# A hybrid attention and MLP block: reordering the head, one load for two input tiles, and a constant folded into a statistics aggregation

## The chip, the cores and the metric

The kernel runs on one core of one Trainium2 chip. A core has a matrix engine (TensorE, "PE" in the profile), a vector engine (VectorE, DVE), a scalar engine (ScalarE, ACT), a general engine (GpSimd, POOL) and an engine that mostly issues transfers (SyncE, SP). They run their own instruction streams and wait for each other by semaphores. Matmuls write PSUM, which has eight banks; DMA engines move data between memory and the on-chip SBUF. The metric is the device time in microseconds of one execution; several are taken and the median is given.

## What is computed

The input x has 2048 rows of 448 numbers. Each row is normalized without learned weights. Two branches start from the normalized rows and both are added to x:

```python
xn = _layernorm(x, axis=-1)                       # (x - mean) / sqrt(var + 1e-5)
return x + _A_ref(xn, ...) + _B_ref(xn, w1, w2)

# A: attention without a softmax over positions, 16 heads of 28
q, k, v = split(xn @ wqkv)
pq, pk  = q @ w_phi, k @ w_phi                    # a 28 x 28 map for each head
phi     = concat(softmax(p), softmax(-p))         # 56 features, for q and for k
kv, z   = sum over rows of phi_k x v, and of phi_k
o       = (phi_q @ kv) / (phi_q . z + 1e-6)
A       = o @ wo
# B: an MLP with 1792 hidden units
B       = silu(xn @ w1) @ w2
```

All inputs and the output are bfloat16.

## The kernel before, in words

Rows are handled in 16 tiles of 128, and tiles in four chunks of 512 rows. TensorE works on halves: each "pair" is two matmuls with 64 contracted rows, one on the upper and one on the lower half of the array, into two neighbouring PSUM banks. Two banks make a slot; there are four, and a list `free` says which slot is taken next (`take`, `give`).

*How the order arises.* The function records operations: `pair` and `tpair` (L446, L459) for matmuls and transposes by matmul, `act` (L464) for ScalarE, `dve` and `pool` for the others, `load` (L477) for transfers. TensorE keeps the recorded order. Other operations are either marked as ordered or placed by `schedule`, a planner with costs and due times for each operation. A wait is put wherever one operation reads or overwrites what another wrote. `schedule` runs at build time; its numbers choose the order and are no measurement.

*The head.* Until the first tile is normalized, TensorE multiplies a matrix of ones (`warm`, ten pairs of 512 columns) into a spare slot. GpSimd writes those ones (L485) after another constant (L484). The input tiles x0 to x3 and `w1` come in on two issuing queues, SP's and ScalarE's; the order of issue is written out by hand (L515 to L524). `w_phi` comes in four small transfers into the block-diagonal tile `BD`, issued on SP after `w1` and ahead of everything in `load_bulk`. The transfers of `load_bulk` (raw query and key weights, value weights, x4 and so on, w2) each wait for the transfer four places before them in the list `chain`.

Tile t is normalized by `LN_st` (statistics, L573), `LN_ag` (aggregation to mean and variance, L577; `ve`, variance plus eps, L579; GpSimd's power of -1/2, `rstd`, L581) and `LN_b` (L596, in pieces). `LN_b` also writes a copy of the first 64 columns behind the tile (columns 448 to 512 of `xnd`), because the lower half of the array reads the columns one block of 64 further than the upper half. `X_tr` transposes the blocks by matmul and `X_ev` copies them out of PSUM, one half by ScalarE and one by DVE.

*The first chunk.* With tiles 0 and 1 transposed for some blocks (`WA`, `WB`), `f1a` and what follows it run the first hidden units of the MLP (F1A, F1B, unit 6) for rows 0 to 255. Then tiles 2 and 3 are transposed and `c0(i, ph)` runs the units for rows 256 to 511. Between them, `FT_tr` transposes the raw query and key weights (T0, T1) and `FM` multiplies them with `BD` (M0 to M3), so that `w_phi` is folded into the query and key weights; both use slot 3. `X_rest` transposes the two blocks of tiles 0 and 1 left over, also in slot 3. `F1silu` applies the activation and frees the slot. After that come the values `V(2)`, `V(0)`, the products with the folded weights (`QK`) and the first output matmuls of the MLP.

*The body* repeats this for chunks 1 to 3 with transposes by DMA. `KV` sums over rows in slot 3.

*The tail.* For tile pairs 0, 2, 4, 6 the MLP output was finished early and lies in `Ye`, in float32 with x added. For pairs 8 to 14 it stays in PSUM: `seed` copies x into the bank, `F2_ph` adds the MLP, and `WO_two` adds the attention output. `U(t)` (called by `nextu`) makes the attention output of a pair, DVE divides it, and a transposing DMA brings it to `oT` (in the profile this tile is part of `E`). `WO(t)` multiplies with `wo` for the early pairs; DVE then adds `Ye` (L833), and `store` writes the result.

Of the kernel before, what the change touches and what calls it, by code (L numbers as in the profile page):

```python
# [140 lines left out]
class _Prog:  # L141
# [97 lines left out]
    def _pass(self, when, shake=0):  # L239
# [46 lines left out]
        while done < n:  # L286
# [20 lines left out]
            if o.is_dma:  # L307
                issue_end = t + o.dur
                eng_free[o.eng] = issue_end
                if o.fixed is not None:  # L310
                    o.end = t + o.fixed
                else:
                    x0 = max(issue_end + 900.0, dma_free[0])
                    dma_free[0] = x0 + o.nbytes
                    o.end = dma_free[0] + 300.0 + o.late
# [14 lines left out]
def bass_parallel_sum__linear_kernel_hedgehog__dense_activation_silu__prompt_kernel(  # L330
# [21 lines left out]
    with es:  # L352
# [23 lines left out]
        st6 = sb("st6", [128, NT, 6], F32)  # L376
        mv = sb("mv", [128, NT, 2], F32)
        ve = sb("ve", [128, NT], F32)
# [8 lines left out]
        wsrc = hT[:, NH - 1, FT - 1, :]  # L387
        ones_bf = wsrc[:, 0:128]
# [84 lines left out]
        def service(nbytes, run):  # L473
            return nbytes / run * (12.0 + 0.0475 * run) / 16.0
# [10 lines left out]
        P.op("pool", 230, lambda e: e.memset(wsrc, 1.0), [], [wsrc], name="ones", ordered=True)  # L485
        P.op("pool", 290, lambda e: e.affine_select(ident[:], ones_bf, [[1, 128]], ALU.is_equal, 0.0, base=0,
                                                    channel_multiplier=-1), [ones_bf], [ident[:]], name="ident", ordered=True)
        def warm(n, sl=2, d=216.0):
            for i in range(n):
                pair([(bank(2 * sl + q)[:, 0:512], ones_bf[HALF[q], :], wsrc[HALF[q], :], True, True) for q in range(2)],  # L490
                     512, "warm", dur=d)

        P.unit = "warm"
        warm(10, d=427.0)


# [3 lines left out]
        def load_x(t0, t1, after=None, eng="sp"):  # L500
            load(x_sb[:, t0:t1, :], xv[:, t0:t1, :], (t1 - t0) * 128 * D * 2, (t1 - t0) * D * 2, f"x{t0}", issue=430, after=after,
                 eng=eng)
# [7 lines left out]
        def load_w1(b, eng):  # L510
            chain.append(load(w1_sb[:, 2 * b:2 * b + 2, :].rearrange("p h f -> p (h f)"), B_w1[b * 128:(b + 1) * 128, :],
                              128 * FF * 2, 2 * FF, f"w1{b}", eng=eng, issue=480))
# [7 lines left out]
        load_x(2, 3, eng="act")  # L520
        load_w1(2, "sp")
        for q, eng in enumerate(("sp", "act")):
            chain.append(load(w1_sb[HALF[q], 6, :], B_w1[384:448, q * 896:(q + 1) * 896], 64 * 896 * 2, 1792, f"w16{q}", eng=eng,
                              issue=480))  # L524
        load_x(3, 4, eng="act")
        P.op("pool", 300, lambda e: e.memset(BD[:], 0.0), [], [BD[:]], name="bd0", ordered=True)
# [3 lines left out]
        wpv = A_w_phi.rearrange("(k q l) d f -> q l d k f", q=2, l=2)  # L530
        wvv = A_wqkv[:, 2 * D:3 * D].rearrange("(s p) c -> p s c", p=64)

        def load_bulk():
# [5 lines left out]

            for b in range(NB):  # L540
                r = 128 if b < 3 else 64
                chained(700.0, wraw[0:r, b, 8:904], A_wqkv[b * 128:b * 128 + r, 0:896], r * 1792, 1792, f"wqk{b}", issue=450)
            for q in range(2):
                chained(2500.0, wv_sb[HALF[q]], wvv, D * D * 2, D * 2, f"wv{q}")
# [7 lines left out]
        for q in range(2):  # L552
            for l in range(2):
                p0 = (64 if q else 8) + l * DH
                load(BD[p0:p0 + DH, :, l * DH:(l + 1) * DH], wpv[q, l], DH * NB * DH * 2, DH * 2, f"wphi{q}{l}", issue=430)

# [4 lines left out]
        def pads_init():  # L561
            for sl in range(NE):
                pads = E[:, sl].rearrange("p k (c n) -> p (k c) n", n=64)[:, :, 56:64]
                P.op("pool", 330, lambda e, pads=pads: e.memset(pads, 0.0), [], [pads], name="pads", ordered=True)
# [5 lines left out]
        def LN_st(t, od=False):  # L570
            P.unit = f"LN{t}"
            xs = x_sb[:, t, :]
            P.op("dve", 630, lambda e: e.bn_stats(st6[:, t, :], xs), [xs], [st6[:, t, :]], name="bnst", ordered=od)  # L573

        def LN_ag(t, od=False):
            P.unit = f"LN{t}"
            P.op("dve", 180, lambda e: e.bn_aggr(mv[:, t, :], st6[:, t, :]), [st6[:, t, :]], [mv[:, t, :]], name="bnag", ordered=od)  # L577
            P.op("dve" if od else "pool", 120 if od else 220,
                 lambda e: e.tensor_scalar(ve[:, t:t + 1], mv[:, t, 1:2], EPS_LN, None, ALU.add),  # L579
                 [mv[:, t, 1:2]], [ve[:, t:t + 1]], name="ve", ordered=od)  # L580
            P.op("pool", 580, lambda e: e.tensor_tensor(rstd[:, t:t + 1], ve[:, t:t + 1], neghalf[:], ALU.pow),  # L581
                 [ve[:, t:t + 1], neghalf[:]], [rstd[:, t:t + 1]], name="rstd", ordered=od)
# [630 lines left out]
```

## Time and profile before

| | |
|---|---|
| median of 13 executions | 149.41 us (148.79 to 150.71) |
| the profiled execution | 148.79 us, with a span of 147.1 us |
| matmul engine busy | 142.3 us, 97% of the span |
| DVE, ACT, POOL busy | 92.3, 88.9, 76.2 us |
| first matmul of the warm-up | 1.39 us |
| first 448-column matmul of `V` | 19.91 us |
| DMA engines busy share, 0 to 5, 5 to 10 us | 0.64, full |

The span runs from the first to the last instruction of the core; the execution's time has a little more around it. Times inside are counted from the span's start. The chain of work goes back from the last instruction, at each step to what released it. A row of the timeline has start, length, engine, line, operation, output and input, and the number of instructions; in brackets stands the idle time before it and what ended it.

### The profile page before, as it was taken

How to read it: one execution, taken by the hardware profiler on the slowest of the kernel's cores; microseconds unless marked ns; L12 is line 12 of the kernel's file. 1: busy time of each engine (PE TensorE's matmuls, PEld its weight loads, DVE VectorE, ACT ScalarE, POOL GpSimd, SP SyncE). 2: the span in 40 equal slices, each digit the busy share in tenths (PEclk: the TensorE clock that was granted, in tenths of full speed). 3: DMA queues.
4: the chain of work that ended last, by engine and by line, in shares of the span. 5: the costliest groups of instructions: out<-in, count | busy, mean ns of one | idle time of the engine just before them, and what ended most of it. 6: DMA issues, size and time to landing. Idle time of an engine off the chain costs nothing.

```text
span 147.1 us, 5049 instructions
## 1 busy us (share of the span) xinstructions
PE 142.3 (97%) x2188; PEld 87.9 (60%) x2188; DVE 92.3 (63%) x176; ACT 88.9 (60%) x119; POOL 76.2 (52%) x87
## 2 busy tenths in 40 slices
PE   6999999999999999999999999999999999999992
PEld 2589975555555555555555556655555555557871
DVE  1877369999986496841067997871067254466632
ACT  4248789997767785975987757598593023040401
POOL 3344025059999959899122999999980000000000
PEclk9999999999999999999999999999999999999999
DMA  4999989855920895359870041333667506314493
GB/s 170 373 245 223 329 249 217 120 97 159 182 58 4 161 179 123 90 126 157 176 152 0 0 104 43 71 76 74 87 131 78 114 4 185 69 65 128 127 135 118
DMA packets 44110, 19.11 MB, mean 130 GB/s; under 512 B 37240, under 2 KB 43448, under 8 KB 44088
## 3 DMA queue, kind: packets, MB, share of 16 engines
q1 hardware_dynamic: 43432, 17.87, 56.0%
q10 hardware_dynamic: 656, 0.92, 1.8%
q8 instruction: 17, 0.28, 0.8%
q14 instruction: 5, 0.04, 0.1%
HBM read 8.17 MB, written 1.84 MB: 68 GB/s over the span
## 4 chain that ended last, share of the span: by engine, by line
PE 93%; DMA 3%; DVE 1%; POOL 0%; issue 0%; ACT 0%; SPq 0%; POOLq 0%
PE psum L446 92%; DMA E<-E 3%; PE psum L459 1%; DVE E L809 1%; POOL hT L485 0%; DVE x_sb L843 0%; ACT xT L464 0%; POOL neghalf L484 0%; SPq L1153 0%; POOLq L1198 0%
## 5 line engine op out<-in xcount | busy, mean ns | idle before, releaser
L713 POOL TENSOR_TENSOR E<-E,Rk 128x896 bf16<-128x896 bf16 x32 | 53.2, 1697 | 7.0 <-DVE Rk L708 5.3
L446 PE MATMUL psum<-xT,w_sb 64*128 64x512 bf16 (+2 forms) x522 | 46.8, 323 | 0.3 <-ACT xT L464 0.3
L446 PE MATMUL psum<-w_sb,hT 64*128 64x448 bf16 (+1 forms) x504 | 45.3, 328 | 0.0
L446 PEld LDWEIGHTS psum<-w_sb,hT 64*128 64x128 bf16 x504 | 25.7, 94 | 16.3 <-ACT psum L464 0.2
L706 DVE TENSOR_REDUCE Sk<-E 128x64 f32<-128x1792 bf16 x16 | 31.9, 2004 | 2.9 <-ACT E L464 2.9
L464 ACT ACTIVATE hT<-psum 128x1024 bf16<-128x1024 f32 (+1 forms) x29 | 28.0, 992 | 8.9 <-PE psum L446 8.5
L446 PEld LDWEIGHTS psum<-xT,w_sb 64*128 64x128 bf16 x522 | 25.1, 94 | 13.9 <-issue 0.4
L464 ACT ACTIVATE E<-psum 128x896 bf16<-128x896 f32 x32 | 27.4, 917 | 6.4 <-PE psum L446 5.2
L446 PE MATMUL psum<-wqk,xT 64*128 64x448 bf16 x224 | 23.7, 349 | 0.0
L446 PEld LDWEIGHTS psum<-wqk,xT 64*128 64x128 bf16 x224 | 12.2, 94 | 8.5
L464 ACT ACTIVATE psum<-x_sb 128x448 f32<-128x448 bf16 (+1 forms) x10 | 4.6, 469 | 20.0 <-PE psum L446 19.4
L581 POOL TENSOR_TENSOR rstd<-ve,neghalf 128x1 f32<-128x1 f32 x16 | 9.1, 569 | 7.2 <-DVE ve L579 6.3
L765 POOL TENSOR_TENSOR Ye<-Ye,x_sb 128x448 f32<-128x448 f32 x8 | 8.2, 1036 | 8.9 <-DVE Ye L763 8.9
L446 PE MATMUL psum<-wo_sb,E 64*128 64x448 bf16 (+1 forms) x126 | 11.9, 328 | 0.2 <-DMA E<-E 0.2
L446 PE MATMUL psum<-wv_sb,xT 64*128 64x448 bf16 x112 | 12.0, 349 | 0.0
L589 DVE TENSOR_SCALAR xnd<-x_sb,mv,rstd 128x896 bf16<-128x896 bf16 x12 | 8.2, 722 | 5.9 <-POOL rstd L581 5.9
L573 DVE BATCH_NORM_STATS2 st<-x_sb 128x6 f32<-128x448 bf16 x16 | 9.5, 604 | 3.2 <-DMA x_sb<-in_A_x_dram 3.1
L763 DVE TENSOR_TENSOR Ye<-psum,Ye 128x448 f32<-128x448 f32 x8 | 5.0, 621 | 10.3 <-ACT Ye L464 10.3
L833 DVE TENSOR_TENSOR x_sb<-psum,Ye 128x448 bf16<-128x448 f32 x8 | 4.8, 607 | 9.7 <-PE psum L446 6.8
L809 DVE TENSOR_TENSOR E<-psum,rden 128x224 bf16<-128x224 f32 x32 | 10.2, 383 | 0.2
L446 PEld LDWEIGHTS psum<-wv_sb,xT 64*128 64x128 bf16 x112 | 5.9, 94 | 3.9
L446 PEld LDWEIGHTS psum<-wo_sb,E 64*128 64x128 bf16 x126 | 5.8, 94 | 4.0 <-DMA E<-E 0.5
(48 smaller groups left out, 99.8 us busy)
## 6 DMA issues: line engine op xcount, KB each, us to landing
w_sb<-in_B_w_dram SPq DMA_DIRECT2D x4, 448.0 KB, 5.3
out_dram<-x_sb SPq DMA_DIRECT2D x7, 224.0 KB, 2.1
w_sb<-in_B_w_dram SPq DMA_DIRECT2D x4, 336.0 KB, 5.2
x_sb<-in_A_x_dram SPq DMA_DIRECT2D x2, 448.0 KB, 4.7
wv_sb<-in_A_wqkv_dram SPq DMA_DIRECT2D x2, 392.0 KB, 5.2
wo_sb<-in_A_wo_dram SPq DMA_DIRECT2D x14, 56.0 KB, 2.2
phT<-in_A_wqkv_dram SPq DMA_DIRECT2D x3, 224.0 KB, 4.0
w_sb<-in_B_w_dram ACTq DMA_DIRECT2D x1, 448.0 KB, 4.3
```

Source lines behind the costliest of these rows:

```text
L446: ins = e.matmul(dst, lhsT, rhs, start=st, stop=sp, skip_group_check=True)
L459: ins = e.transpose(dst, src, idn)
L464: return P.op("act", d_act(n), lambda e: e.activation(dst, src, func, scale=scale), reads=reads or [src], writes=writes or [dst], table=ta ...
L573: P.op("dve", 630, lambda e: e.bn_stats(st6[:, t, :], xs), [xs], [st6[:, t, :]], name="bnst", ordered=od)
L581: P.op("pool", 580, lambda e: e.tensor_tensor(rstd[:, t:t + 1], ve[:, t:t + 1], neghalf[:], ALU.pow), [ve[:, t:t + 1], neghalf[:]], [rstd[ ...
L589: dve(lambda e: e.tensor_scalar(dst, src, mv[:, t, 0:1], rstd[:, t:t + 1], ALU.subtract, ALU.mult), 734, [src, mv[:, t, 0:1], rstd[:, t:t ...
L706: dve(lambda e: e.tensor_reduce(Sk[:, t % 3, :].rearrange("p (h g) -> p h g", g=2), Er, AXL.X, ALU.add), d_dve(1792), [Er], [Sk[:, t % 3, ...
L713: pool(lambda e, Eh=Eh, Rb=Rb: e.tensor_tensor(Eh, Eh, Rb, ALU.mult), 1770, [Eh, Rh], [Eh], "phi%d" % qk)
L763: dve(lambda e: e.tensor_tensor(y, b, y, ALU.add), d_dve(D), [b, y], [y], "ye_d")
L765: pool(lambda e: e.tensor_tensor(y, y, x_sb[:, t, :], ALU.add), 1110, [y, x_sb[:, t, :]], [y], "ye_x")
L809: dve(lambda e, dst=dst, src=src, rb=rb: e.tensor_tensor(dst, src, rb, ALU.mult), d_dve(224), [src, r], [dst], "o")
L833: dve(lambda e, bk=bk, y=y, dst=dst: e.tensor_tensor(dst, bk, y, ALU.add), d_dve(D), [bk, y], [dst], "out")
```

## The change

The diff combines edits in several places.

- Loads: x2 and x3 become one transfer on ScalarE's queue behind a block of `w1`. The four `w_phi` transfers move from SP's queue to ScalarE's. The list `chain` gains the new transfer, so the transfers of `load_bulk` wait for other ones than before.
- Normalization: `st6` has nine columns instead of six. The last three are set once so that the aggregation itself adds eps to the variance, and `ve` is removed for all tiles.
- Warm-up: the ones are 128 columns written by DVE; the matmul reads them four times over. Nine pairs instead of ten.
- The copies of 64 columns of tiles 0 and 1 are made later. Until then zeros stand in their place, and `X_rest` transposes that block too.
- First chunk: the units run in a new order. F1A's sixth block and F1B interleave, X(2) comes inside F1B, X(3) after the first half of unit 6; unit 6 takes all 512 rows with one activation; the first `c0` is split by tile. Slot 3 joins the rotation until KV needs it.
- Tail: `WO` seeds the bank with `Ye` by two ScalarE copies and leaves by one ScalarE and one DVE copy. U(6) comes inside F2 of pair 12 and U(14) inside WO(4). In `F2_ph` the place of `mid` is 6 by default instead of 3.
- Costs of the planner are altered, which can reorder operations that are not marked as ordered.

```diff
-        st6 = sb("st6", [128, NT, 6], F32)
+        st6 = sb("st6", [128, NT, 9], F32)
-        P.op("pool", 230, lambda e: e.memset(wsrc, 1.0), [], [wsrc], name="ones", ordered=True)
+        P.op("dve", 100, lambda e: e.memset(ones_bf, 1.0), [], [ones_bf], name="ones", ordered=True)
...
+        P.op("pool", 100, lambda e: e.memset(xnd[:, 0:2, D:512], 0.0), [], [xnd[:, 0:2, D:512]], name="xz", ordered=True)
+        P.op("dve", 90, lambda e: e.memset(st6[:, :, 6:9], 0.0), [], [st6[:, :, 6:9]], name="eps0", ordered=True)
+        P.op("dve", 90, lambda e: e.memset(st6[:, :, 8:9], D * EPS_LN), [], [st6[:, :, 8:9]], name="eps", ordered=True)
-        warm(10, d=427.0)
+        warm(9, d=427.0)
...
-        load_x(2, 3, eng="act")
         load_w1(2, "sp")
+        chain.append(load(x_sb[:, 2:4, :], xv[:, 2:4, :], 256 * D * 2, 4 * D, "x2", eng="act", issue=430))
         for q, eng in enumerate(("sp", "act")):
             chain.append(load(w1_sb[HALF[q], 6, :], B_w1[384:448, q * 896:(q + 1) * 896], ...
-        load_x(3, 4, eng="act")
...
+        for q in range(2):
+            for l in range(2):
+                p0 = (64 if q else 8) + l * DH
+                load(BD[p0:p0 + DH, ...], wpv[q, l], ..., f"wphi{q}{l}", eng="act", issue=500)
...
-            P.op("dve" if od else "pool", 120 if od else 220,
-                 lambda e: e.tensor_scalar(ve[:, t:t + 1], mv[:, t, 1:2], EPS_LN, None, ALU.add),
-                 [mv[:, t, 1:2]], [ve[:, t:t + 1]], name="ve", ordered=od)
...
-        LN_b(0, ((0, 256), (256, D), (D, 512)), True)
+        LN_b(0, ((0, 256), (256, D)), True)
...
+        for h in range(2):
+            P.unit = "F1A"
+            for u in range(2):
+                F1ph(0, sa[h], u * 256, 2 * h + u, 0, 256, False, ())
+            F1silu(sa[h], 2 * h, 0, 0, 256, 2)
+            P.unit = "F1B"
+            for u in range(2):
+                F1ph(h, sb_, u * 256, 4 + u, 0, 256, h == 0 and u == 0)
+                if h == u == 0:
+                    X_tr(2, 3, range(NS))
+                    X_ev(2, 3, range(NS), True)
+        F1silu(sb_, 4, 0, 0, 256, 2)
+        def x3():
+            X_tr(3, 3, range(NS))
+            X_ev(3, 3, range(0, 4))
+            X_ev(3, 3, range(4, 7), False, 256)
+            give(3)
...
+        for name, k in (("U0", 0), ("X3", 0), ("U1", 1), ("A", 1), ("60", 0), ("B", 0), ("X", 1), ("61", 0), ("T0", 0),
+                            ("01", 0), ("20", 0), ("M0", 0), ("21", 0), ("40", 1), ("M1", 0), ("T1", 0), ("41", 0), ("V0", 0),
+                            ("M3", 1), ("M2", 0), ("V2", 0)):
+            if k:
+                free.insert(0, free.pop(k))
+            head[name]()
...
-        def WO(t, ub):
+        def WO(t, ub, mid=None):
             sl = take()
-            WO_mm(t, ub, sl, 0, D, False)
+            P.unit = f"WO{t}"
+            for q in range(2):
+                act(bank(2 * sl + q)[:, 0:D], Ye[:, (t + q) % NYE, :], ACTF.Identity, D, name="seed")
+            WO_mm(t, ub, sl, 0, D, mid)
...
-                dve(lambda e, bk=bk, y=y, dst=dst: e.tensor_tensor(dst, bk, y, ALU.add), d_dve(D), [bk, y], [dst], "out")
+                if q:
+                    dve(lambda e, bk=bk, dst=dst: e.tensor_copy(dst, bk), d_dve(D), [bk], [dst], "out")
+                else:
+                    act(dst, bk, ACTF.Identity, D, name="out")
...
-        ph1(12, 0, D)
-        nextu(6)
+        F2_ph(12, sls[12, 0], 1, 0, D, lambda: nextu(6), 8)
         ph0(14, 0, M)
-        wo2(4, 12)
+        WO(4, ub[4], lambda: nextu(14))
+        WO_two(12, ub[12], sls[12, 0], 0, D)
```

In the new order A and B are the first `c0` for tile 2 and for tile 3, U0 and U1 are unit 6 for rows 0 to 255 in its two phases, 60 and 61 the same for rows 256 to 511, two digits otherwise are unit and phase of `c0`, and X is `X_rest`.

## The prediction

> **What bounds the kernel now.** I read the page first, then the chain of waits in order of time, then the timelines of single engines around each gap of the chain, and last the landing times of the head's loads. The page:
>
> ```profile
> span 147.1 us, 5049 instructions
> PE 142.3 (97%) x2188; PEld 87.9 (60%) x2188; DVE 92.3 (63%) x176; ACT 88.9 (60%) x119; POOL 76.2 (52%) x87
> PE 93%; DMA 3%; DVE 1%; POOL 0%; issue 0%; ACT 0%; SPq 0%; POOLq 0%
> ```
>
> TensorE is the bound nearly everywhere, so a change counts only where it starts TensorE's real work earlier, closes a gap in its stream, or adds or removes matmuls. The chain (start us, length us, what) says where gaps are:
>
> ```profile
> 0.88 0.47 POOL hT L485
> 1.39 4.45 PE psum L446 x10
> 5.84 0.13 PE psum L459 x4
> 5.97 0.02 issue
> 5.99 0.29 ACT xT L464
> 6.28 0.14 issue
> 6.41 0.51 PE psum L446 x8
> ...
> 12.78 0.47 PE psum L459 x32
> 13.25 0.03 issue
> 13.28 4.96 PE psum L446 x111
> ...
> 138.48 4.20 DMA E<-E
> 142.69 0.05 issue
> 142.73 1.53 PE psum L446 x28
> ```
>
> Ends of matmuls are modelled, so a gap is measured from starts. Four gaps follow. (a) The ten warm-up pairs hold TensorE to 5.63, where the timeline shows the first transposes start; their normalized data were ready at 5.48, the weight load's start. (b) 32 weight transposes start at 12.62. X(2)'s 14 took 0.20, so 32 take 0.46; the next matmul starts at 13.28: 0.20 lost, waiting for ScalarE's copy of X(3) (12.59 + 0.54, then 0.14 to reach TensorE). (c) X_rest: the last five 256-column matmuls run from 19.29, so the last pair starts near 19.51 and should be followed at 19.62; X_rest starts at 19.79. 0.17 lost, put down to DVE's copy of the weight transposes out of bank slot 3. (d) 28 matmuls of 224 columns start at 141.03 and the next group at 142.73: 1.70. The same 28 at 132.63 were followed at 133.97: 1.34. So 0.36 lost on the transposing DMA of tile pair 14. Between 20 and 142 us no start is late by more than a few hundredths.
>
> The loads that the head waits for, and DVE's work on them:
>
> ```profile
> 7.87 0.63 DVE L573 BATCH_NORM_STATS2 st<-x_sb 128x6 f32<-128x448 bf16 x1
> 8.53 0.18 DVE L577 BATCH_NORM_AGGREGATE mv<-st 128x2 f32<-128x6 f32 x1
> 8.75 0.15 DVE L579 TENSOR_SCALAR ve<-mv 128x1 f32<-128x1 f32 x1
> 8.97 0.63 DVE L573 BATCH_NORM_STATS2 st<-x_sb 128x6 f32<-128x448 bf16 x1
> ```
>
> The landing times of the single issues: x0 3.1, x1 3.4, w1 blocks 5.15, 5.64, 7.4, x2 7.82, the last w1 rows 8.2 and 8.5, x3 8.96. Both statistics start at their tile's landing.
>
> **What the skill says.** "TensorE: Matmul & The Clock Gate", Part 1: the array runs at half clock until about 3.4 us of sustained work. The trace agrees: ten 512-column pairs take 4.45 (0.427 a pair from start to start), the eight 128-column matmuls at 6.41 take 0.51, and sixteen at 6.98 take the same 0.51. Its section on the back-to-back gap prices a warm matmul at N/2.4 + 2.5 ns: 55.8 ns for 128 columns, 109.2 for 256. The 88 matmuls at 7.58 are 20 pairs of the first and 24 of the second, 3.74 by the price, 3.81 in the chain. "DMA: Bandwidth & Descriptors", section on queues and rings: a DMA engine alternates between the issuing queues packet by packet. From 5.2 to 6.7 us the DMA view has 156 packets of SP's queue beside 150 of ScalarE's, at 376 GB/s. No page prices the rest; it is from rows.
>
> **Part by part, against the profiled execution's 148.79 (span 147.1).**
>
> Start. `ones` is now 128 columns on idle DVE instead of 512 on GpSimd behind `neghalf`: GpSimd began at 0.78, so DVE can be done near 0.96 and TensorE start at 1.02, not 1.39. Nine pairs end at 1.02 + 9 x 0.427 = 4.86. The data: statistics of x0 3.14 to 3.77, aggregation 3.80 to 3.98, and without `ve` (0.15, and 0.09 to cross) the power runs 4.07 to 4.62. DVE has statistics of x1 from about 3.9 to 4.5 and its aggregation to 4.72; the first normalization starts about 4.75, not 5.03. The old distance of 0.45 gives the weight load 5.20, transposes 5.23, not 5.63: **-0.40**. f1a moves from 6.41 to 6.01; its w1 blocks landed at 5.15 and 5.64. If DVE starts late, up to 0.4 of slack (4.86 against 5.23) covers it.
>
> w_phi on ScalarE. Its four issues follow at 2.86. On SP four took 1.96, so ScalarE is free near 4.9 and its first copy comes at 5.59. If each took as long as x3's 0.78, it is free at 5.98, which costs 0.4. SP's w_qk waits now hang one transfer later (w1's third block, 7.4 to 7.7, instead of 5.64), and wv, x4, w2, x6 queue behind them. Cover: T0 needs w_qk at 14.6 (it landed at 9.7 to 10.4), V0 needs wv at 19.6 (15.5), w2 is needed from 25 us. A microsecond late costs nothing.
>
> The new unit order. X(2) moves up by ten pairs: TensorE is there at 7.58 - 0.40 + 20 x 0.0615 + 14 x 0.109 = 9.94 (before, 11.2). Its data: x2 and x3 now land together. The extra 112 KB alternates with w1's block, and at 376 GB/s that is 0.30, so landing at 8.1; bounds are 7.82 (x2 as before) and 8.96 (x3 as before). From the landing: statistics +0.05, aggregation +0.71, second statistics +0.80, its aggregation +1.46, normalization (448 columns, 0.42) +1.56, 0.11 to TensorE: +2.1, thus 10.2. **+0.28**; bounds 0 and 1.1. X(3) follows 0.20 + 16 x 0.109 later at 12.15. Its evacuation starts 0.50 on (12.65), in two steps per engine; ScalarE's 256 columns lie between 192 (0.33) and 448 (0.54), say 0.39, so 13.18 with the crossing, the second step 13.51. Unit 60 needs both, at 13.13 and 13.40 (three pairs and eight short ones after X(3)): **+0.16**, bounds 0 and 0.4.
>
> Gaps (b) and (c) go: T0 no longer follows X(3), and with slot 3 in rotation X_rest sits behind X(3)'s copy, finished half a microsecond before: **-0.20 - 0.17**. Later slots: U0 on the first silu (about 1.0, finished 1 us before), T0 on silu of F1B (14.55 against 14.65), QK0 on V0's copy (0.3 spare). All thin but whole.
>
> TensorE's own work: 16 pairs of 128 for 8 of 256, 16 x 55.8 - 8 x 109.2 = **+0.02**; two more transposing pairs **+0.06**.
>
> Chunk 1. DVE takes statistics of tiles 6 and 7 after the FM copies, so the last x transposing DMA goes out near 29.0 (before 28.97), lands near 32.3; TensorE needs it at about 33.2 (before 33.5). Spare 0.9. Twelve GpSimd `ve` at 0.22 vanish under its idle time.
>
> Tail. Pair WO now adds Ye by two ScalarE seeds and leaves by one ScalarE and one DVE copy. ScalarE gains 8 x 0.54 + 4 x 0.54 = 6.5 us where it was busy 6.9 of 30. Tightest is WO(6): seeds 138.25 to 139.3 plus 0.14, TensorE at 139.70; without that cover it costs what it is late. U(14) moves ahead of three pairs (0.57) and its DVE work loses one 0.6 us add ahead of it. DVE: den 135.35, rden to 135.93, the WO(4) copy 135.97 to 136.55, four products 1.27: 137.82, not 138.43. The DMA lands 0.6 earlier, 142.1 against a need of 142.37: **-0.36**.
>
> Sum: -0.40 + 0.28 + 0.16 - 0.20 - 0.17 + 0.02 + 0.06 - 0.36 = **-0.61**. The profiled execution is the fastest of those shown, 0.62 under the median; from the median 149.41 the same sum gives **148.8**.
>
> **Rivals.** *The joint transfer takes the gain.* x2 and x3 land where x3 did, X(2) stalls 1.1: sum +0.2, 149.6; at a landing of 8.5 it is 149.2. For it: the pair is behind a whole w1 block. Against: in 5.2 to 6.7 ScalarE's packets got every second turn.
>
> *The tail transposing DMA doesn't move.* It took 4.2 where the median is 2.7; if what delays it stays, -0.25 remains: 149.15. Against: DVE's operations ahead of it are plainly fewer.
>
> *Slower: the clock stays low.* Before, dense work pauses from 5.63 to 6.41 (0.78), and full clock still comes by 6.98. After, the pause runs from 4.86 to 6.01, 1.15. If that is too much for a window, the next 3.4 us run at half rate, doing 1.7 us of work: +1.7, less the 0.28 and 0.16 that hide under it and part of the pause already paid: about 150.0. It decides from a pause between 0.78 and 1.15.
>
> **How the numbers follow.** The sum with landings up to 8.3: 0.55. Joint transfer late: 0.18. Tail unmoved, or a thin slot failing (about 149.1): 0.14. Low clock: 0.13. Within 0.3%, about what this measurement can tell from no change, means 148.96 to 149.86. Faster is the first case and a little of the second and third: 0.60; within: 0.27; slower: 0.13. The likeliest case alone spans 148.3 (no X(2) stall) to 149.0; to leave out no more than two in ten the range goes from 148.2 to 149.7.
>
> **What would show it.** First warm-up matmul near 1.0 and transposes near 5.2; one stall of about 0.3 before X(2), under the DVE normalization of tile 2; x2 landing near 8.1; T0 and X_rest without a wait; no wait for the E DMA at the end, WO(14) starting 1.34 after the group before it. Wrong would be: 128-column matmuls 0.1 apart beyond 7 us, a landing past 8.5, or a new TensorE wait on a ScalarE silu or seed.

## The result and the profile after

The changed kernel takes 150.99 us (median of 11 executions, 149.74 to 152.15) against 149.24 for the kernel before (48 executions): a ratio of 1.0119, 95% interval 1.0093 to 1.0146. It is slower by 1.2%, 1.8 us. The prediction said 148.8 us, with a range of 148.2 to 149.7, and gave slower a chance of 0.13. Ratios leave out executions that took over 1.5% longer than the fastest of their kernel, and so do the medians given below for kernels cut off behind the head. The profiled execution of the changed kernel took 150.99 us with a span of 149.3, 2.2 us above the span before.

The page of the changed kernel: the span, the engines' busy times, the queue of instruction transfers (packets, MB, share), and the shares of the chain:

```profile
span 149.3 us, 5104 instructions
PE 141.6 (95%) x2206; PEld 104.8 (70%) x2206; DVE 89.8 (60%) x174; ACT 94.6 (63%) x131; POOL 73.0 (49%) x75
...
q8 instruction: 17, 0.28, 0.8%
...
PE 90%; DMA 5%; DVE 2%; issue 1%; ACT 0%; ACTq 0%
```

TensorE is busy 0.7 us less than before in a span 2.2 us longer: it stands still 2.9 us more. "Issue", time in which an engine waits for nothing that the profile shows, has become 1% of the chain. The line of q8 says what will matter: the instructions themselves arrive by DMA, in 17 blocks of 0.28 MB / 17 = 16 KB. The chain of waits in order of time (start, length, what):

```profile
1.84 7.28 DMA x_sb<-in_A_x_dram
...
9.15 0.64 DVE st L576
...
10.74 0.34 DVE xnd L596
...
11.12 0.41 PE psum L457 x14
11.54 1.76 PE psum L444 x32
13.30 0.20 PE psum L457 x14
13.51 1.73 PE psum L444 x46
15.23 0.17 PE psum L457 x12
15.41 0.33 PE psum L444 x6
15.74 0.47 PE psum L457 x32
16.20 2.63 PE psum L444 x59
18.84 1.69 issue
20.52 1.05 PE psum L444 x25
```

X(2)'s 14 transposes start at 11.12, behind the joint transfer that landed at 9.12. From there X(3), X_rest and T0 (the rows with 14, 12 and 32 transposes) follow without a pause: gaps (b) and (c) of the prediction are gone. Then TensorE stops for 1.69 us, and the profile shows nothing that released it. From start to start the gap is 18.57 to 20.52, 1.85 more than the matmul's own length.

DVE's rows for tiles 2 and 3, which answer those of before:

```profile
9.15 0.63 DVE L576 BATCH_NORM_STATS2 st<-x_sb 128x6 f32<-128x448 bf16 x1 [1.51 <-DMA x_sb<-in_A_x_dram]
9.81 0.20 DVE L580 BATCH_NORM_AGGREGATE mv<-st 128x2 f32<-128x9 f32 x1
9.92 0.58 DVE L576 BATCH_NORM_STATS2 st<-x_sb 128x6 f32<-128x448 bf16 x1
10.54 0.20 DVE L580 BATCH_NORM_AGGREGATE mv<-st 128x2 f32<-128x9 f32 x1
```

TensorE's timeline at the start, around the stop and at the end (start, length, engine, line, operation, count, and in brackets the idle time before it with what ended it):

```profile
1.12 3.62 PE L444 MATMUL psum<-hT 64*128 64x512 bf16 x18 [1.12 <-DVE st L493]
5.25 0.41 PE L457 MATMUL psum<-ident,xnd 64*128 64x64 bf16 x10 [0.51 <-DVE xnd L596]
6.68 0.40 PE L444 MATMUL psum<-xT,w_sb 64*128 64x128 bf16 x8 [1.02 <-DMA w_sb<-in_B_w_dram]
...
17.79 1.04 PE L444 MATMUL psum<-xT,w_sb 64*128 64x256 bf16 x15
20.52 0.92 PE L444 MATMUL psum<-xT,w_sb 64*128 64x256 bf16 x13 [1.69 <-issue]
...
143.60 1.51 PE L444 MATMUL psum<-w_sb,hT 64*128 64x224 bf16 x28
144.94 1.51 PE L444 MATMUL psum<-wo_sb,E 64*128 64x224 bf16 x28
```

The warm-up and the transposes start where they were expected (5.25); f1a waits for w1 until 6.68; the end has no wait for E any more (143.60 to 144.94 is 1.34).

From the starts of the matmuls, the 2.2 us are: f1a at 6.68 instead of 6.41, +0.27; its first eight matmuls in 0.22 instead of 0.33, because full clock came at 4.20 here and at 6.68 before, -0.11; a wait for w1's third block at 8.69, +0.24; X(2), +0.59; the stop, +1.85; a few more short pairs, +0.08 by the prediction's price; the three gaps that closed, -0.20 - 0.17 - 0.36. Sum +2.19.

What happens while TensorE stands still, against the time before it (window, its length, busy time and count of each engine, TensorE's granted clock, DMA share, GB/s):

```profile
14.20:18.60 4.40, 4.40 (x139) 4.18 (x133) 2.77 (x9) 3.50 (x5) 0.76 (x5) 1.00 1.04 254
18.60:20.50 1.90, 0.23 (x5) 0.00 (x0) 0.76 (x2) 1.07 (x2) 0.00 (x0) 1.00 1.05 362
```

The other engines are half idle too, and the DMA engines are full in both windows. One packet among them is a block of instructions: it started at 18.07, landed at 19.15, and TensorE went on 1.37 us later.

### The profile page after: what moved, and what is told of

The parts are those of the page before. It is cut to its first block, busy times and chain, and to the rows that moved or that the text cites. A ratio compares the mean times of both kernels' runs of the same rounds, so it can differ in the third digit from the quotient of the medians.

```text
span 149.3 us, 5104 instructions
## 1 busy us (share of the span) xinstructions
PE 141.6 (95%) x2206; PEld 104.8 (70%) x2206; DVE 89.8 (60%) x174; ACT 94.6 (63%) x131; POOL 73.0 (49%) x75
## 4 chain that ended last, share of the span: by engine, by line
PE 90%; DMA 5%; DVE 2%; issue 1%; ACT 0%; ACTq 0%
PE psum L444 88%; DMA x_sb<-in_A_x_dram 5%; PE psum L457 1%; DVE st L576 1%; ACT L516 0%; ACTq L475 0%; DVE x_sb L853 0%; DVE mv L580 0%; DVE xnd L596 0%
## 5 line engine op out<-in xcount | busy, mean ns | idle before, releaser
L444 PE MATMUL psum<-xT,w_sb 64*128 64x512 bf16 (+2 forms) x538 | 47.7, 318 | 2.8 <-issue 1.7
L444 PEld LDWEIGHTS psum<-xT,w_sb 64*128 64x128 bf16 x538 | 30.1, 94 | 12.1 <-issue 2.2
L444 PEld LDWEIGHTS psum<-w_sb,hT 64*128 64x128 bf16 x504 | 30.4, 94 | 11.6
L462 ACT ACTIVATE hT<-psum 128x1024 bf16<-128x1024 f32 x28 | 28.3, 1022 | 10.8 <-PE psum L444 9.9
L444 PE MATMUL psum<-wqk,xT 64*128 64x448 bf16 x224 | 24.2, 349 | 0.0
L444 PEld LDWEIGHTS psum<-wqk,xT 64*128 64x128 bf16 x224 | 16.6, 94 | 4.3
L462 ACT ACTIVATE x_sb<-psum 128x448 bf16<-128x448 f32 (+1 forms) x12 | 5.8, 511 | 19.5 <-PE psum L444 11.8
L581 POOL TENSOR_TENSOR rstd<-mv,neghalf 128x1 f32<-128x1 f32 x16 | 8.7, 560 | 18.6 <-DVE mv L580 18.6
L766 DVE TENSOR_TENSOR Ye<-psum,Ye 128x448 f32<-128x448 f32 x8 | 5.0, 621 | 10.9 <-ACT Ye L462 10.8
L444 PEld LDWEIGHTS psum<-wv_sb,xT 64*128 64x128 bf16 x112 | 8.2, 94 | 1.9
L841 DVE CAST x_sb<-psum 128x448 bf16<-128x448 f32 x4 | 2.4, 609 | 9.8 <-PE psum L444 9.8
```

What stands on the lines that cost most here:

```text
L444: ins = e.matmul(dst, lhsT, rhs, start=st, stop=sp, skip_group_check=True)
L462: return P.op("act", d_act(n), lambda e: e.activation(dst, src, func, scale=scale), reads=reads or [src], writes=writes or [dst], table=ta ...
L766: dve(lambda e: e.tensor_tensor(y, b, y, ALU.add), d_dve(D), [b, y], [y], "ye_d")
L841: dve(lambda e, bk=bk, dst=dst: e.tensor_copy(dst, bk), d_dve(D), [bk], [dst], "out")
```

## The experiments

Theory, formed on this trace: TensorE ran out of instructions; the next block queued behind bulk transfers, and the new order used up the block before it sooner. Rivals: a wait on data or a bank that the records don't name; the edit of the loads as the cause of all; the order of the units as such. Hole means the gap of TensorE's starts beyond a matmul's own length. "Instruction 704" counts, from 0, all that the trace shows of TensorE from the program's start: matmuls, weight loads and the few records of its sequencer (13 to 16 up to there). Without those records the count ahead of the hole is not the same in all kernels: 689 in those with the order of before, 691 or 692 in the others.

### Does the hole belong to the work or to the count?

```diff
-  warm(9)    # 9 pairs of 512 columns
+  warm(18)   # 18 pairs of 256 columns: the same time, 36 instructions more
```

> The changed kernel with its 9 warm-up pairs of 512 columns made 18 pairs of 256: the same columns and time, but 36 more TensorE instructions ahead of the work (18 pairs more matmuls and weight loads), all else instruction for instruction the same. Two readings of the 1.85 us hole at 18.67 to 20.52 us. Fetch reading (TensorE ran out of instructions, the block of 16,384 bytes landed at 19.15 only): the hole stays at the same count of instructions from the program's start (about 704 visible ones), so it comes 36 instructions earlier in the work, some 0.8 to 1.2 us earlier, with a length of 1 to 2.5 us; 150.3 to 151.6 us. Data reading (the matmul behind the hole waits for data or a bank that the records don't name): the hole stays ahead of the same 256-column matmul, at about 18.6 to 20.5 us; 150.9 to 151.1 us.

153.29 us, ratio 1.0235 (1.0156 to 1.0314), above both readings. The timeline of TensorE:

```profile
17.28 0.34 PE L444 MATMUL psum<-BD,phT 64*128 64x56 bf16 x13
20.55 0.21 PE L444 MATMUL psum<-BD,phT 56*128 56x56 bf16 x3 [2.92 <-issue]
```

The hole moved away from the 256-column matmul into the middle of a group of sixteen with the same operands, and it is still behind instruction 704. New data can hardly be awaited there: the three that wait read the same tiles as those just ahead of them. In all kernels below that have a hole, whatever their order, it stands behind the same instruction, 704. So the supply of instructions is the cause; the data reading is out. The hole was longer than expected, 3.08 us, and a stretch of half clock followed it (next run).

### Which part of the change brings it?

The loads put back, everything else changed:

```diff
+        load_x(2, 3, eng="act")          # ahead of w1's third block
         load_w1(2, "sp")
-        chain.append(load(x_sb[:, 2:4, :], ...))
...
+        load_x(3, 4, eng="act")          # last; w_phi back on SP's queue
```

> The changed kernel with the loads of the head as they were: x2 and x3 two transfers with x2 ahead of w1's third block and x3 last, w_phi on SyncE's queue; start, order and tail as changed. If the new loads are what delayed w1 and x2: the three head stalls (0.27 for w1's first blocks, 0.24 for its third, 0.59 for X(2)) come to 0.3 or less together, w_qk and wv come a microsecond earlier, and the fetch hole shrinks to 0 to 0.8 us because the transfers around it end earlier; 148.2 to 149.3 us. If the order of the units alone makes the hole: 1.3 to 1.9 us of it stays, 149.6 to 150.2 us. If the lateness of w1 was a chance of that one execution: the head stalls vary without the loads, 150.5 to 151.1 us.

151.86 us, ratio 1.0163 (1.0086 to 1.0240): none of the three. Only one head wait was left (0.69 before X(2)), but the hole grew to 2.30 us, and TensorE's clock fell behind it. Windows of this kernel (length, busy time and count of TensorE, clock, DMA share, GB/s):

```profile
18.00:20.00 2.00, 0.46 (x9) 1.00 1.07 366
20.00:22.00 2.00, 1.40 (x21) 0.69 0.80 272
22.00:24.00 2.00, 2.00 (x51) 0.50 0.08 22
24.00:26.00 2.00, 2.00 (x46) 0.95 0.11 15
```

The clock's shortfall, 2 x 0.31 + 2 x 0.50 + 2 x 0.05, is another 1.7 us. After the 3.08 us hole the clock fell in the same way; after the 1.85 us one it did not. So the hole comes without the new loads too.

The loads edit alone, on the kernel before:

```diff
-        load_x(2, 3, eng="act")
         load_w1(2, "sp")
+        chain.append(load(x_sb[:, 2:4, :], xv[:, 2:4, :], ..., eng="act"))
...
+                load(BD[...], wpv[q, l], ..., eng="act")   # was on SP's queue
```

> The kernel before with the loads edit alone: x2 and x3 one transfer behind w1 on ScalarE's queue, w_phi behind that. If the new loads delay w1 and x2: f1a starts 0.2 to 0.3 us later than its 6.41, X(2) waits 0.4 to 0.8 us for the joint transfer landing near 9, the second block of instructions comes late in the kernel's order too and adds 0 to 0.6 us; 149.8 to 150.9 us. If only the lateness of that one execution showed there: x2 lands near 8.1 and the sum is 0 to 0.4 us; 149.2 to 149.7 us.

149.85 us, ratio 1.0027 (0.9999 to 1.0055), a loss that is not clear of noise. In its profile the joint transfer landed at 8.26 and X(2) did not wait; the hole was 1.16 us, where the kernel before has none.

Start and tail alone and together, on the loads and order of before (the diffs are those of the change):

> The kernel before with the start edits alone (ones on VectorE, nine warm-up pairs, eps inside the aggregation, no ve). By the prediction's first step the transposes start at 5.23 instead of 5.63 and f1a at about 6.0, -0.40 us: 148.8 to 149.0 us against 149.3. If w1's first block sets f1a instead: f1a at 6.4 to 6.7, 0 to -0.1 us. Fetch reading: a hole of 0 to 1.5 us at the 704th visible TensorE instruction (near 18 us) in this as in every kernel with this order, the same as before on average; if the head runs 0.4 us earlier and the block's landing does not, up to 0.4 of the gain is given back.

149.28 us, ratio 0.9987 (0.9959 to 1.0015), no gain that can be told. In the profile, of an execution of 150.64 us, w1's second block landed at 7.85 only, and the hole was 0.70.

> The kernel before with the tail edits alone (sums of the last row blocks seeded by ScalarE, U(6) and U(14) in the middle of other units, so the last transfer of E starts earlier). By the prediction's last step the wait of WO(14) for its E goes: -0.36 us, 148.85 to 149.05 us against 149.3. Rival: TensorE loses the same again at the new places of U, 149.2 to 149.5 us.

148.39 us, ratio 0.9955 (0.9931 to 0.9980): the tail's gain is real, and this is the best of all whole kernels run, better than both kernels of the study. Its profile has no hole.

> The kernel before with the start and the tail edits, loads and order as they were. If both gains hold and add: -0.6 to -0.76 us, 148.5 to 148.75 us against 149.3. If the hole at the 704th instruction takes the start's gain back: 148.9 us.

149.16 us, ratio 0.9983 (0.9958 to 1.0007). Its chain of waits:

```profile
12.12 0.47 PE psum L457 x32
12.59 4.94 PE psum L444 x112
17.53 0.06 PE psum L457 x4
17.59 0.93 issue
18.52 0.51 PE psum L457 x18
```

TensorE is at instruction 704 at 17.40, in the kernel before at 18.08. The block of instructions landed at 16.97 here and at 16.84 there, so all of the head start, 0.68, goes into the hole (1.10), and more. The kernel before passes this place just in time: 1.37 after landing, the delay seen in the changed kernel, is 18.21, and its next matmul started at 18.20.

### Order or count?

```diff
-  U0 X3 U1 A 60 B X 61 T0 01 20 M0 21 ...    # A, B: unit 0,0 in two halves of 128 columns
+  U0 X3 U1 T0 60 00 X 61 01 20 M0 21 ...     # 00: the unit in one piece (loads as before)
```

> The changed start and tail, the loads of before, and the changed order of chunk 0 with two moves: the weight transposes T0 come right behind U1 in place of the two 128-column halves A and B of unit 0,0, which become one unit of 256 columns. From the widths of the matmuls, TensorE passes its instructions 448 to 704 (the third block of 256) in 5.3 us here, 4.2 us in the changed kernel and 5.0 us in the one before. Fetch reading (request to use takes some 5.1 to 7.0 us): the hole is 0 to 1.5 us, a microsecond less than the 2.3 us of the changed kernel with old loads, and TensorE's clock stays whole; 148.4 to 149.5 us. If the order as such is to blame rather than the count: hole of 1.5 us or more, over 150 us.

150.68 us, ratio 1.0080 (1.0050 to 1.0109), missed in time. The hole shrank as expected, from 2.30 to 0.89, and the clock stayed whole, but T0 waited 0.56 at its new place, X_rest 0.58 for DVE's copy, and the last transposing transfer was late by 0.37 again, although this kernel has the tail edits.

### Why is the block late?

First w2 and x6 alone were held back:

```diff
   w2_part(0, 4); w2_part(4, 7); x_pair(6); ...
+  # each of these also waits for TensorE to have done unit 21
```

> The changed kernel with the loads of w2 and of x6, and so the rest of w1 behind them on SyncE's queue, held until TensorE has done the unit 21 (about 17.5 us); w_qk, wv and x4 as they are. Fetch reading (the block of instructions waits behind bulk transfers): the second block lands by 17 us, no hole over 0.4 us between 17 and 21 us; 149.1 to 149.6 us, and up to 0.4 more if w2 is late for its first use near 26 us. If the hole has nothing to do with the transfers: it stays at 1.5 to 1.9 us, 150.8 to 151.2 us.

150.74 us, ratio 1.0078 (1.0048 to 1.0108). The hole went from 1.85 to 1.45 only, so the gain expected from this reading did not come. Packets of wv and then x4 filled the DMA engines until 17.25 us, and the block started at 17.19, as they ran out. The next three kernels hold x4 as well, and earlier.

```diff
+  mk = mark()          # TensorE behind the first half of unit 2,0
   x_pair(4); w2_part(0, 4); ...
+  # each also waits for mk
```

> The kernel before with one change: the loads behind wv (x4, w2, x6, and so the rest of w1) are held until TensorE has done the first halves of units 0,0 and 2,0 (about 15 us); work and order of TensorE as they were. In the runs so far the second block of instructions starts 2.4 to 4.3 us after TensorE passed its 460th visible instruction (about 13.0 us here), under bulk transfers. Fetch reading (the fetch queues behind them): it starts by 14.7 us and lands by 16 us, the 704th instruction shows no hole, and with the holes that other executions of this kernel have the median falls by 0.3 to 0.9 us: 148.4 to 149.1 us against 149.4. If the fetch doesn't mind the transfers: landing near 16.8 us as now, 149.2 to 149.6 us; w2 late for its first use near 24 us would show as a wait there, up to 0.5 us.

149.30 us, ratio 1.0000 (0.9980 to 1.0020): no hole in the profile, but no gain in the median either. The profile is of an execution of 151.62 us, in which w1's second block landed at 8.21 and TensorE ran at half clock from 7.63 to 11.04; as the kernel before has no hole in its profile either, this run says little.

> Start and tail edits of the change on the loads and order of before, with x4, w2, x6 held until the first halves of units 0,0 and 2,0 are done (about 14.5 us). Without the hold the profile had 1.12 us of hole at the 704th instruction. Fetch reading: block landed by 15.5 us, no hole, 1.1 us off that profile's 146.9: span 145.8 to 146.2, median 147.8 to 148.3 us against 149.4. If the fetch doesn't mind the transfers: the hole stays at 0.8 to 1.5 us, 149.0 to 149.3 us.

148.85 us, ratio 0.9971 (0.9946 to 0.9995). The hole went from 1.10 to 0.23 in the profile; of the 1.1 to 1.6 us expected against before, 0.4 came. In the profile TensorE lost 0.66 us to w1's third block in the head, and 0.7 near 34.9 us behind ScalarE's copy into `Ye`, which the kernel without the hold did not lose; whether the held loads delayed that copy was not looked into.

> The changed start, order and tail with the loads of before, and x4, w2, x6 held until TensorE has done the unit 20 (about 16 us). Without the hold: hole of 2.3 us at the 704th instruction, then a stretch of lower clock, 151.9 us. Fetch reading: TensorE passes the third block in 4.2 us here; request to use takes 3.5 to 4.8 us with the queues emptier, so a hole of 0 to 0.6 us, the clock stays whole, and the start, gap and tail gains of the prediction appear: 148.0 to 149.0 us. If the fetch doesn't mind the transfers: hole of 1.5 us or more, 150.5 us or more.

149.50 us, ratio 0.9990 (0.9960 to 1.0020), where the same kernel without the hold had 1.0163. Its chain of waits across the place:

```profile
16.17 0.47 PE psum L457 x32
16.64 3.50 PE psum L444 x88
20.14 0.40 PE psum L457 x22
```

No hole, no fall of the clock behind it, and by the medians 2.4 us less than without the hold. The block of instructions started at 15.88, just as the last packets of wv (there were some 60 in a quarter of a microsecond until 15.75, 48 then, 12 at 16.0) ran out. So the block seems to have waited for wv; the next runs test that.

The 148.0 to 149.0 us that were expected did not come, and the trace shows why: TensorE ran at half clock far into the head. The same groups of 128-column matmuls in the changed kernel and then here:

```profile
7.03 0.62 PE L444 MATMUL psum<-xT,w_sb 64*128 64x128 bf16 x16
7.48 0.25 PE L457 MATMUL psum<-ident,xnd 64*128 64x64 bf16 x6
...
6.70 1.07 PE L444 MATMUL psum<-xT,w_sb 64*128 64x128 bf16 x16
7.54 0.39 PE L457 MATMUL psum<-ident,xnd 64*128 64x64 bf16 x6
```

From start to start sixteen take 0.84 here and 0.45 there. Pairs of 128 columns are 0.107 apart here, against 0.056, and those of 256 columns 0.213, against 0.109, until 10.1 us. (The clock column says 1.00 for this run, but its trace has no record of the clock at all.) x2 landed at 8.93, which by the 2.0 us that the changed kernel took allows X(2) at 10.9; it started at 11.60, behind TensorE's own work, where the prediction had 10.2. These 1.4 us are more than the gains of start and gaps together (0.77). How often the clock stays low so long is not shown; the 14 executions run from 147.84 to 150.91 us.

To hold wv itself, the kernels were cut behind the head; the expectations say what they leave out. Some stores of the output start within the head there.

```diff
+  mk = mark()          # TensorE behind U1 (changed order), behind unit 6,0 (order of before)
   chained(2000.0, wv_sb[HALF[q]], ...)
+  # waits for mk; x4, w2, x6 follow behind it in the queue
```

> The first 25 us of the changed kernel, TensorE's instructions one for one as they are, up to the second V; left out is all behind it (queries and keys, attention, the second layer, chunks 1 to 3, and so every transposing transfer). In its place stand 60 pairs of 512-column matmuls on ones (12.8 us) and the stores, so the output is rows of x. It is the base for the next run. Both readings: the hole at the 704th visible TensorE instruction is there, 1.4 to 2.4 us, second block landing near 19 us; about 41 to 44 us in all.

> The same cut-off head with one change: wv and all bulk loads behind it (x4, w2, x6, the rest of w1) are held until TensorE has done U1 (about 13.1 us), so that nothing large is queued when TensorE enters the second block near 14 us. If the fetch queues behind the bulk transfers: it starts within 1.5 us of the 460th visible instruction, lands by 16.5 us, no hole over 0.2 us, and the time is 1.4 to 2.2 us under the run before, unless wv is late for V(0) at 19 to 20 us, which gives back up to 0.7. If the block takes that long whatever is queued: hole of 1.4 us or more, the same time.

40.92 us without and 39.71 us with the hold (lowest 40.73 and 39.45; spans of the profiles 39.2 and 37.7), 1.2 us less. Windows around TensorE's way to the block's edge, columns as in the windows of the changed kernel (length, TensorE, its weight loads, DVE, ScalarE, GpSimd, clock, DMA share, GB/s), first without the hold:

```profile
14.00:14.90 0.90, 0.90 (x32) 0.79 (x26) 0.18 (x2) 0.90 (x3) 0.90 (x6) 1.00 0.92 248
16.00:18.00 2.00, 2.00 (x67) 1.99 (x61) 1.88 (x7) 1.90 (x2) 0.00 (x0) 1.00 1.12 247
18.00:20.00 2.00, 0.92 (x16) 0.58 (x12) 0.62 (x1) 1.57 (x2) 0.00 (x0) 1.00 1.06 298
```

and with it:

```profile
14.00:14.90 0.90, 0.90 (x33) 0.79 (x28) 0.00 (x0) 0.90 (x2) 0.77 (x5) 1.00 0.16 60
16.00:18.00 2.00, 2.00 (x53) 1.97 (x50) 1.72 (x7) 1.71 (x3) 0.00 (x0) 1.00 1.07 269
```

With little on the DMA engines at 14 to 14.9 us (share 0.16) the block started at 15.17, 0.66 us after instruction 460; with 0.92 and more at 18.18, 3.4 us after. (460 is a mark: in none of these traces did the block that is missing behind 704 start before TensorE was there.) The hole of 2.09 us is gone. wv is then late for V(0) by 0.93, which gives part of it back, as the chain shows:

```profile
14.39 6.86 DMA wv_sb<-in_A_wqkv_dram
...
21.39 16.09 PE psum L444 x172
```

The same in the order of before with the start edits:

> The first 23 us of the kernel before with the start edits, cut off in the same way (the same parts left out, the same 60 pairs behind). Hole at the 704th instruction of 0.5 to 1.5 us, as in the two whole kernels with these edits (0.7 and 1.1).

> That one with wv and all behind it held until unit 6,0 is done (about 12.3 us). If the fetch queues behind the bulk transfers: block landed by 15.3 us, no hole, 0.5 to 1.2 us faster than the run before. If the hold only moves the wait to V(2): the same time.

38.10 and 37.89 us (lowest 37.93 and 37.80), inconclusive in time: in the profile there was no hole without the hold either, the block having landed at 16.11. With the hold it landed at 14.91; it started 1.00 us after instruction 460 instead of 2.03, so here too the hold brings the block forward. No whole kernel with wv held gave a time, so what that is worth there stays open. So does how the block comes to wait, where the prediction counts on DMA engines that alternate between the queues: the runs show when it starts, and not why.

For most kernels in one table, from the records of the traces: when TensorE starts instruction 460, when the block starts and lands, how long the start comes after instruction 460, how long TensorE takes from 460 to 704, and the hole.

```
kernel                    460th  block starts, lands  after  460 to 704  hole
before                    12.97  15.77  16.84          2.80     5.11     0.01
before_tail               12.94  15.38  16.75          2.44     5.11     0.01
before_loads              12.87  16.52  17.83          3.66     5.06     1.16
before_start              13.97  17.04  18.32          3.07     5.06     0.70
before_start_tail         12.34  15.70  16.97          3.36     5.06     1.10
before_quiet              15.56  16.73  17.69          1.18     5.06     0.05
before_start_tail_quiet   13.54  15.87  17.16          2.33     5.06     0.23
order_balanced            13.86  18.12  19.24          4.27     5.79     0.89
after                     14.72  18.07  19.15          3.35     3.85     1.85
after_shift               13.74  17.73  19.18          3.99     3.71     3.08
after_late_bulk           14.49  17.19  18.32          2.70     3.85     1.45
after_old_loads           14.34  18.01  19.13          3.67     3.85     2.30
after_old_loads_quiet     15.15  15.88  17.20          0.73     3.85     0
front_after               14.80  18.18  19.47          3.38     3.85     2.09
front_after_wv            14.52  15.17  16.58          0.66     3.85     0
```

For the changed kernel: 3.35 + 1.08 (the transfer) + 1.37 (landing to the next instruction) is 5.80 after instruction 460, against 3.85 that the work lasts: a gap of 1.95, of which 0.11 is the matmul itself. In the kernel before the same sum is 5.24 against 5.11. In the balanced order the 5.79 hold the wait of X_rest, 0.58.

### What the loads edit costs by itself

> The cut-off head of the changed kernel with wv held, once more (the same parts left out), as the partner of the next run: no hole at the 704th instruction, 39.5 to 40.0 us, X(2) waiting 0.5 to 0.8 us for the joint transfer of x2 and x3.

> The same head and hold with the loads of before: x2 and x3 apart, x2 ahead of w1's third block, w_phi on SyncE's queue (the same parts left out). If the joint transfer behind w1 costs what the prediction's second step says: X(2) waits 0.2 to 0.5 us less than in the partner and the time is 0.2 to 0.5 us less. If w1's and x2's landings vary by chance as much as the edit moves them: within 0.2 us of the partner, with X(2) waiting 0.3 us or more here too.

39.67 and 39.25 us. The old loads are 0.4 us faster, as the first reading said (the medians of all six executions, 40.25 and 39.48, are 0.8 apart), though X(2) did not wait less and a hole of 1.35 us came back with them: TensorE was at U1 a microsecond earlier there and the hold released wv before the block was fetched. In the head, the new loads made TensorE wait 0.96 for w1's third block and 0.49 before X(2); the old ones 0.76 before X(2). Over all profiles of the study, w1's third block landed at 8.58 on average with the new loads (7 profiles, 7.52 to 9.12) and at 7.97 with the old (12, 7.33 to 9.14); the joint transfer at 8.94 (8.26 to 9.31), and x2 alone at 8.42 (7.65 to 9.31). w1's first two blocks landed alike with both. These averages are over different kernels; with the pair they put the cost of the edit in the head near half a microsecond, while chance moves these landings by more than a microsecond.

## Why the prediction was wrong, step by step

The sum said -0.61, and the profiled execution came out at +2.20, 2.81 apart. The stop is 1.85 of it, f1a 0.67, X(2) 0.31 and w1's third block 0.24; X(3) and the earlier full clock give 0.16 and 0.11 back.

**Start, -0.40: right, but not at f1a.** The weight load came at 5.22 and the transposes at 5.25 (predicted 5.20 and 5.23). f1a was to follow at 6.01; it waited for w1 until 6.68, because the step took the landings of before (5.15 and 5.64) as given. They were 6.54 and 6.73 in this profile; with the loads of before they were anywhere in 4.7 to 6.4 and 5.6 to 8.2 in 12 profiles.

**The chain of loads, "a microsecond late costs nothing": incomplete.** It listed what needs the data, and left out that the instructions come over the same DMA engines. wv went out at 11.45 instead of 9.73, and the loads edit alone has a hole of 1.16 us in its profile. But the hole is no shorter with the old loads (2.30 us, wv at 10.51), so this was not the main cause.

**TensorE's own work, +0.02 and +0.06: the step that failed.** It priced 16 pairs for 8, and two more transposing pairs, by the time in the array. In instructions the first is 32 more and the second 8 more, with the four of the warm-up pair less: 36 more by the end of the head. The new order, above all, put X_rest, T0 and half B of unit 0,0 (128 columns) into the stretch from 460 to 704, where 49 matmuls of 256 columns are left of 80. So TensorE passes it in 3.85 us, not 5.11, and the block of instructions took 5.8 us from the same mark to TensorE's going on. 1.85 us was lost and no term of the sum could hold it. No row of the profile before shows a wait there; but its trace has the block's packets and shows that the block came only as TensorE got there, and that was not looked at.

The Trainium skill, "Runtime: NRT & Kernel Launch", section "Instruction fetch mechanics", says that an engine's instructions come in blocks of 16 KiB, 256 instructions, over a DMA queue of their own, and that the cost of crossing a boundary is mostly hidden. The block's size agrees with the trace (17 packets of 16 KB for 4,412 matmuls and weight loads). That the hole stands at an edge between blocks, three times 256 with TensorE's unrecorded waits counted, is argued and not shown. That the cost is hidden does not hold here: up to 3.08 us.

**X(2), +0.28: the mechanism right, the size off.** The joint transfer landed at 9.12, not 8.1, outside the range of 7.82 to 8.96 that the step gave and past the 8.5 that it named as a sign of being wrong; the stall was 0.59. From landing to TensorE it took 2.0 (predicted 2.1). Behind the same traffic w1's third block cost another 0.24 that no step had.

**X(3), +0.16: too high.** The trace has no late start behind X(3); U1 and the half unit A cover its copies.

**Gaps, -0.37, and tail, -0.36: right.** All three are gone from the trace, and the tail alone is 0.45% faster on the chip (0.20 to 0.69), 0.7 us with 0.36 inside the interval.

**The rivals.** The low clock after the pause ahead of f1a did not come in the changed kernel's profile, though f1a came later than feared (6.68): its records have full clock from 4.20 on, inside the warm-up. In the profile with old loads and x4 held it did come, and lasted to 10.1. So that rival was a fair one, and a single profile does not decide it. Nor does the kernel before bear out the figure behind it: full clock came there at 6.68, 5.3 us after the first matmul and not 3.4 (in the changed kernel 3.1 us after it). The late joint transfer came in part, the unmoved tail not at all. The slower side, to which 0.13 was given, was reached by a mechanism that none of them had.

## What to carry to other kernels

Count instructions and not only columns: where TensorE goes through some 245 instructions in less than the 5.2 to 6.8 us that a block took here behind bulk transfers, from instruction 460 to TensorE's going on, ask for the block of instructions; the trace has its packets, and "issue" on the chain of an engine that should be dense is its sign. A bulk load that may come late in its own right can still hold up the instructions. To hold it back until the block is under way took the hole away in two kernels (2.30 and 2.09 us); longer matmuls there shortened it (2.30 to 0.89) and cost as much elsewhere. Landings taken from a single profile can be a lucky draw; here they vary by more than a microsecond from one execution to another.

## What the runs showed that was not expected

- In kernels with holes of 0.2 to 3.1 us, all stand behind instruction 704 of those that the trace shows; TensorE goes on 1.3 to 1.7 us after the block has landed.
- The block starts 0.66 us after instruction 460 with nearly empty DMA engines and 2.0 to 4.3 us after it where no load was held; its transfer takes 1.0 to 1.5 us.
- Starting the head 0.68 us earlier gained nothing in the profile with start and tail edits, because the block's landing did not move (16.97 against 16.84).
- Full clock in the head came by 7.2 us in all profiles but one, as early as 3.9, and in that one at 10.1, though the first matmul always starts between 1.1 and 1.4.
- Holes of 2.30 and 3.08 us near 18 us were each followed by 3.4 us at half clock, one of 1.85 us and, in the cut-off head, one of 2.09 us were not. In the head, after shorter pauses had gone before, 1.4 us of waiting were enough for it (`before_quiet`, from 7.63). The Trainium skill, "TensorE: Matmul & The Clock Gate", Part 1, ties the clock to recent activity, which agrees; a length of pause that is always tolerated does not come out of these runs.
